# One batch of six token tiles for GT's last blocks, in a kernel that mixes linear attention with a gated linear unit

## The chip, the cores and the metric

The kernel runs on one core of one Trainium2 chip. The metric is the device time of one launch in microseconds (us), smaller is better. The engines are called PE (TensorE), ACT (ScalarE), DVE (VectorE), POOL (GpSimd) and SP (SyncE, which here only starts transfers). SP and POOL each start the transfers of one queue.

## The reference, cut to what matters

The input x has 2048 tokens of 640 values. One branch is linear attention with 32 heads of 20 values, the other a gated linear unit with an inner width of 1536; a gate per token mixes the two.

```python
phi = lambda t: where(t > 0, t + 1, exp(t)) + 1e-6
kv  = einsum("bhsd,bhse->bhde", phi(k), v)
z   = einsum("bhsd->bhd", phi(k))
num = einsum("bhqd,bhde->bhqe", phi(q), kv)
den = einsum("bhqd,bhd->bhq", phi(q), z) + 1e-6
a   = (num / den) @ wo
b   = (sigmoid(x @ w_gate) * (x @ w_up)) @ w_down
g   = sigmoid(sum(x * gate_w))
return g * a + (1 - g) * b
```

All of it is in 32 bit.

## The kernel before, in words

**Arithmetic.** Each operand of a product is split into a high and a low part (names in h and l: xth and xtl, woh and wol). `mm3` makes a product from three matmuls, at lines L407, L408 and L409 of the profile: high by high, low by high, high by low. ACT writes the high part (L420) and DVE subtracts to get the low part (L424). The large products use seven forms, sums of blocks of the operands, in place of eight block products; such sums of weights are made on DVE (the wst, qraw rows), split, and stored to DRAM by POOL (wq, wf, wd) for later use.

**k and GT.** v is never formed. Phase 1 goes through four chunks c = 0 to 3 of two blocks of 256 tokens. For each block PE makes k, ACT and DVE apply phi (tiles kr and kb, tag "kr", five buffers), and the split gives token tiles tok (`token_tile`, L492), which hold x and phi(k), high and low, for 128 tokens. POOL adds phi(k) to zacc by an accumulating transfer. `GTBatch` (L1013) adds x^T phi(k) over its token tiles, in seven units u, each in its own PSUM bank (five of 512 columns, one of 384 and one of 256), and `out` adds the bank to gt in SBUF on DVE. `batches` gives each chunk the blocks whose tiles are batched, and block 7 has a batch of its own, glast. `gt_turn` and `gt_back` then turn the columns of gt that stand past the 512th, through DRAM.

**From GT to m.** For six groups of heads hg, `kv_part` makes kv = Wv^T GT in ten matmul records (L1619; wv_sb, three buffers, loaded by `load_mv`), and DVE keeps the blocks of its heads (kvt, kvh, kvl). `wo_split` makes woh and wol from wo_sb (two buffers, `load_mo`), and asks for the load of hg+2. `m_part` multiplies kv by Wo and copies the bank to ms, with ACT, or for hg 4 with DVE (L866). These parts are spread over the slots of `q_phase(1, ...)`, which computes phi(q) for half of the columns (units ch, cc, dd with weights ws, wu, wg), by the list `extra`.

**The order.** The class `Order` (L31) plans the program at build time: pieces of ACT and DVE work wait in lists (the "qw" items among them, which sum and split the weights of the q and down products), and `fill`, `need` and `run` put them between PE's units. The order that results is fixed on each engine. An engine waits for the semaphores of its next instruction and holds back all that stands behind it, and so does SP with its loads. `queue_s` (L1320) splits the weights ws; behind the second half of each split `order.then(load_w)` places the next load of a wst tile, which has two buffers.

**Queues and PSUM.** PSUM has tiles by tag: ch, cc, dd, rot. A tile can only be written anew when its reader (ACT or DVE) is done.

Of the kernel before, what the change touches and what calls it, by code (L numbers as in the profile page):

```python
# [7 lines left out]
F32 = mybir.dt.float32  # L8
F32R = mybir.dt.float32r
# [5 lines left out]
P = 128  # L15
# [359 lines left out]
def gated_mix_kernel(ctx: ExitStack, tc: tile.TileContext, xt, xn, wk, wv, wo, wst_q, wst_f, out_t):  # L375
# [115 lines left out]

    def token_tile(dt=F32R):  # L492

        early = len(tok_n) % 6 < 4
        tok_n.append(0)
        return p1.tile([P, 4, D], dt, name="tok", tag="toka" if early else "tokb", bufs=4 if early else 2)

    p1.tile([P, HW], F32, name="first", tag="ta", bufs=2)
    warm = nc.const_aps.tensor(1.0, (P, 512), mybir.dt.bfloat16)
# [180 lines left out]
    chunks[0].b12 = (b12h, b12l)  # L680
    xt_dram = dram.tile([P, 4, 2, 2, CW], F32, name="xt_dram")
    p1.tile([P, 48], F32, name="shift")
    st = [token_tile(F32).rearrange("p a b -> p (a b)") for _ in range(2)]
    wk_st = [st[k // 3][:, k % 3 * 2 * HW:(k % 3 + 1) * 2 * HW] for k in range(KC)]
    k3h, k3l = (p1.tile([P, 2, HW], F32R, name=n, tag="kr", bufs=5) for n in ("k3h", "k3l"))
    p1.tile([P, 472], F32, name="space")

    nc.scalar.dma_start(wk_st[0][:, :HW], wk[:P, :HW])
    for k in range(KC):
# [434 lines left out]
        g.part(u, 0, 2, "rot" if u % 2 else "dd")  # L1124
        order.fill()
    order.slack(False)
    batches = {1: [1, 2], 2: [3, 4], 3: [5, 6]}

    for c in range(1, 4):
        ck = chunks[c]  # L1130
        if c == 1:
            queue_qw(2)
        a, b = KBlock(2 * c), KBlock(2 * c + 1)
        for n in range(1, 6):
            order.need((ck, n))
            if c == 1 and n >= 3:
                order.need(("ks", (1, 0, 2)[n - 3]))
            getattr(a, f"s{n}")()
            getattr(b, f"s{n}")()
            for _ in range(({1: 1, 2: 1, 3: 1, 5: 1}, {3: 2, 4: 2, 5: 2})[c - 2].get(n, 0) if c > 1 else 0):  # L1140
                order.run("qw")
        order.need((ck, 6))
        if c == 1:
            order.need(("ks", 5))
        if c == 2:
            chunks[c + 1].load()
        elif c == 3:
            nx = [Chunk(1, i, None, i * CW, xst_v, (b12h, b12l)) for i in range(2)]
            nx[0].load()
        if c == 1:  # L1150
            order.need(("xn", 1))
        queue_xn(2 * c)
        a.s6()
        a.s7()
        a.sum_b()
        a.phi_a()
        b.s6()
        a.phi_b()
        order.need(("pk", 2 * c - 1))
        k_split(tok(2 * c, 0))  # L1160
        b.s7()
        b.sum_b()
        k_split(tok(2 * c, 1))
        if c == 3:
            order.need("qw")
            qs_cm.__exit__(None, None, None)
            pa_cm.__exit__(None, None, None)
            px_cm = tc.tile_pool(name="px", bufs=1, side="right", reuse_waits="tile")
            px = px_cm.__enter__()
            xf = XForms(px, TG)  # L1170
            pg_cm = tc.tile_pool(name="pg", bufs=1, side="right", reuse_waits="tile")
            pg = pg_cm.__enter__()
            pz_cm = tc.tile_pool(name="pz", bufs=1, side="right", reuse_waits="tile")
            pz = pz_cm.__enter__()
            z = pz.tile([P, 8, CW], F32, name="xz", tag="ws")
            z0 = m1_tile("ma", "xm")[:, :2 * CW].rearrange("p (k c) -> p k c", c=CW)
            nx[1].x = (Rows((0, 2, z0), (2, KC, z[:, 0:3])), z[:, 3:8])
            nx[1].load(((0, 0, 2), (0, 2, KC), (1, 0, KC)))
            W, WT = {}, {}

            def wg_tile():
                return pg.tile([P, 2, D], F32R, name="wg", tag="wg", bufs=2)

            def put(n, i, t):
                WT[n, i] = t
                W[n, i] = [t[:, c] for c in range(2)]

            def store_w(n, i):

                key = n[::2] + (i,)  # L1190
                w_dram[key] = dram.tile(list(WT[n, i].shape), F32, name="w%s%d%d" % key)
                gp.dma_start(w_dram[key], f32(WT[n, i]))

            def wg_split(n, src):
                put(n, 0, wg_tile())
                split(*W[n, 0], src)
                if n[0] == "f" or n[2] == 0:
                    order.then(lambda: store_w(n, 0))
            nx[0].f = nx[1].f = xf
            put(("q", 1, 2), 0, wg_tile())  # L1200
            sp.dma_start(f32(WT[("q", 1, 2), 0]), w_dram["q", 2, 0])
        g = GTBatch(c, batches[c])
        if c > 1:
            order.need(("xn", 2 * c))
        if c == 1:
            chunks[1].store_t(1, 0)
        elif c < 3:
            chunks[c + 1].queue()
        else:
            queue_xn(7)  # L1210
        first = 4 if c == 1 else 3
        for u in range(first):
            g.part(u, 0, 2, ("rot", "dd", "ch", "cc")[u])
            if c == 1 and u == 0:
                order.need(("xn", 2))
                chunks[1].store_t(2, 3)
                chunks[2].queue()
            if u == (c == 1):
                b.phi_a()
            if u == 1 + (c == 1):  # L1220
                b.phi_b()
                order.ahead(5)
        queue_split(2 * c + 1)
        if c < 3:
            queue_xn(2 * c + 1)
        else:
            w_stage = m1_tile("ma", "w0")
            sp.dma_start(w_stage, wst_q[:, KC - 1])
            queue_forms(nx)
        for u in range(NU):  # L1230
            g.part(u, 2 if u in g.ps else 0, len(g.tiles), ("rot", "dd", "ch", "cc", "dd", "rot", "rot")[u])
            order.fill()
            if u in (2, 3, 4, 6):
                order.run("qw")
            if c == 2 and u == NU - 1:
                queue_ls()
    order.need(("xn", 7))
    glast = GTBatch(4, [7])
    tags = ["ch", "dd", "dd", "cc", "cc", "rot", "ch"]

    for u in (KC, KC + 1, 0):
        glast.part(u, 0, 2, tags[u])
    order.add(0, v_cost(D), gt_turn, "turned", first=True)
    for u in range(1, KC):
        glast.part(u, 0, 2, tags[u], out=False)
        order.fill()
        if u == 1:
            wg_split(("q", 1, KC - 1), w_stage)
        elif u == 3:
            glast.out(1)  # L1250
    p1_tail = [lambda u=u: glast.out(u) for u in range(2, KC)] + [lambda: order.need("turned")]
    p1_cm.__exit__(None, None, None)

    pw_cm = tc.tile_pool(name="pw", bufs=1, side="right", reuse_waits="tile")
# [291 lines left out]
            for g in gs2:  # L1546
                order.add(0, v_cost(TG), lambda g=g, u=u: one(g, u), "den", lambda g=g, u=u: order.when(st[g, u]) + 1.5, chain=True)

    sp.t = max(sp.t, z_started[-1][0])
    load_w()  # L1550
    mp_cm = tc.tile_pool(name="mp", bufs=1, reuse_waits="tile")
    mp = mp_cm.__enter__()
# [6 lines left out]
    def load_mv(hg):  # L1559
        if hg < NHG:  # L1560
            c0, w = hg_slice(hg)
            v = mp.tile([P, KC, bdn], F32, name="wv_sb", tag="wv_sb", bufs=3)
            sp.dma_start(v[:, :, :w], wv.rearrange("(k p) c -> p k c", p=P)[:, :, c0:c0 + w])
            MV[hg] = v

    def load_mo(hg):
        if hg < NHG:
# [46 lines left out]
    def kv_part(hg, tag="ch"):  # L1614
        c0, w = hg_slice(hg)
        v = MV[hg]
        ps = ps_tile(tag)
        for m in range(KC):
            nc.tensor.matmul(ps[:w, :w], v[:, m, :w], gt[:, m, c0:c0 + w], start=(m == 0), stop=(m == KC - 1))  # L1619
        order.on_pe(10, 2 * bdn)  # L1620
        kvt = mp.tile([bdn, bdn], F32, name="kvt", tag="kvt", bufs=2)
        vec2(kvt[:w, :w], ps[:w, :w], bd.rearrange("p b c -> p (b c)")[:w, :w], OP.mult, "p")
        kvh = mp.tile([bdn, bdn], F32R, name="kvh", tag="kvh", bufs=3)
        kvl = mp.tile([bdn, bdn], F32R, name="kvl", tag="kvl", bufs=3)
        vec_copy(kvh[:w, :w], kvt[:w, :w])
        vec2(kvl[:w, :w], kvt[:w, :w], f32(kvh[:w, :w]), OP.subtract)
        KV[hg] = (kvh, kvl)
        load_mv(hg + 3)
# [15 lines left out]
        queue_wo(hg + 2)  # L1644

    load_mv(0)
    sp.t = max(sp.t, order.pe + P_LAG)
    load_mv(1)
    load_mv(2)
    load_mo(0)  # L1650
    load_form(("q", 1, 2), 2)
    load_mo(1)
    load_form(("q", 1, 2), 1)

    down_pool, down_cms = [], []
# [823 lines left out]
    extra[13].append(lambda: order.need(("wg", ("f", 1, 0)), False))  # L2479
    extra[13].append(lambda: order.need(("w", ("f", 1, 0), 0), False))  # L2480
    extra[14].append(lambda: order.need(("w", ("f", 1, 0), 1), False))
    for hg, (j, t) in enumerate(((1, "rot"), (1, "rot"), (3, "cc"), (6, "rot"), (9, "rot"), (10, "rot"))):
        extra[j].append(lambda hg=hg, t=t: kv_part(hg, t))
    extra[8].append(gt_back)
    extra[12].append(z_perm)
    extra[15] += [z_sum, m_close]
    q = q_phase(1, lambda k: [(b12h[:, k], b12l[:, k])], extra)
# [524 lines left out]
def _layout(inputs):  # L3012
# [8 lines left out]
    wk = wqkv[:, D:2 * D]  # L3021
    wk = np.concatenate([wk[:, :HALF], gw, gw, wk[:, HALF:], gw, gw], axis=1)

    def cols(w):
        return np.ascontiguousarray(w).reshape(KC, P, FC, P).transpose(2, 1, 0, 3).reshape(FC, P, D)

    wst_f = np.stack([cols(inputs["B_w_gate"]), cols(inputs["B_w_up"]),
                      np.ascontiguousarray(inputs["B_w_down"]).reshape(FC, P, D)], axis=2)
    arrays = {
        "xt": xt, "xn": x, "wk": wk, "wv": wqkv[:, 2 * D:],  # L3030
        "wo": np.ascontiguousarray(inputs["A_wo"]), "wst_q": wst_q, "wst_f": wst_f,
    }
    return {k: np.ascontiguousarray(v) for k, v in arrays.items()}
# [15 lines left out]
```

## Time and profile before

| | us |
|---|---|
| median of 3 runs | 727.34 |
| lowest and highest run | 726.14, 727.4 |
| the profiled execution | 729.87 |
| span of its trace (first to last instruction) | 728.0 |
| PE busy | 719.7 |
| DVE busy | 587.0 |
| ACT busy | 370.5 |
| POOL busy | 116.4 |

The profiled execution is one execution of its own, slower than the three timed runs. In the rows of the timeline stand the start from the span's beginning in us, the duration, the engine, the line and operation, the tiles out<-in, the shape, the count, and in brackets the idle time before the instruction and what ended it. In the rows of waits stand the waiting engine and tile, the releaser, and then the total us, the number of times and the longest. In the rows of windows stand the stretch, its length, then for each engine the busy time with a count, PEclk (the granted TensorE clock, 1.00 is full speed), the share of the DMA engines, and GB/s. Names are as the program has them, with buffer numbers left out.

### The profile page before, as it was taken

The numbers are of one execution on the slowest core, as the hardware profiler recorded it, in microseconds if no ns is written. First come the engines' busy times: TensorE is split into PE (matmuls) and PEld (weight loads), VectorE is DVE, ScalarE is ACT, GpSimd is POOL, SyncE is SP. The second block draws the span as 40 slices with busy tenths as digits, with TensorE's granted clock in tenths as the row PEclk, the third lists the DMA queues.
The fourth block names the chain that finished last, engine by engine and source line by source line (L and its number), as shares of the span: only waits on it lengthen the run. The fifth ranks groups of instructions, "written<-read, shape, count | busy, mean of one in ns | idle before, by whom it ended". The sixth has DMA issues, their size and how long they took to land.

```text
span 728.0 us, 9897 instructions
## 1 busy us (share of the span) xinstructions
PE 719.7 (99%) x3395; PEld 607.4 (83%) x3395; DVE 587.0 (81%) x1016; ACT 370.5 (51%) x685; POOL 116.4 (16%) x189
## 2 busy tenths in 40 slices
PE   9999999998999999999999999999999999999998
PEld 8999998887888888888888888888888888888886
DVE  6898887986678889898989977347696968799895
ACT  5784749166556763635354754355423241444451
POOL 0211012222320221311211134001010101002300
PEclk9999999999999999999999999999999999999999
DMA  7677679798867866767677979968989895959957
GB/s 250 166 207 202 178 183 295 196 294 277 295 225 274 317 229 241 259 222 274 265 295 283 297 270 345 413 245 280 346 267 308 258 392 178 408 215 337 220 104 236
DMA packets 81960, 191.93 MB, mean 264 GB/s; under 512 B 12234, under 2 KB 40346, under 8 KB 78198
## 3 DMA queue, kind: packets, MB, share of 16 engines
q1 hardware_dynamic: 60726, 117.72, 49.6%
q0 software_dynamic: 20896, 73.36, 30.2%
q8 instruction: 26, 0.43, 0.2%
q14 instruction: 24, 0.20, 0.1%
q10 hardware_dynamic: 288, 0.23, 0.1%
HBM read 113.46 MB, written 75.52 MB: 260 GB/s over the span
## 4 chain that ended last, share of the span: by engine, by line
PE 90%; DVE 4%; issue 2%; DMA 2%; POOL 1%; ACT 0%; SPq 0%; DVEq 0%; POOLq 0%; ACTq 0%
PE ch L407 10%; PE ch L409 10%; PE ch L408 10%; PE cc L407 8%; PE cc L408 8%; PE cc L409 8%; PE dd L407 6%; PE dd L408 6%; PE dd L409 6%; PE rot L407 5%; PE rot L409 5%; PE rot L408 5%; DMA qraw<-wst_f 1%; DVE xtl L424 1%; DVE gt L424 1%
## 5 line engine op out<-in xcount | busy, mean ns | idle before, releaser
L420 ACT ACTIVATE c<-ch 128x512 f32<-128x512 f32 x54 | 32.2, 597 | 94.5 <-PE ch L409 93.7
L424 DVE TENSOR_TENSOR hf<-c,hf 128x512 fp32r<-128x512 f32 x80 | 54.4, 686 | 19.3 <-ACT hf L420 18.9
L420 ACT ACTIVATE hf<-c 128x512 fp32r<-128x512 f32 x80 | 48.9, 625 | 31.1 <-DVE c L424 31.1
L424 DVE TENSOR_TENSOR c<-cc,c 128x512 f32<-128x512 f32 x42 | 28.9, 688 | 26.9 <-PE cc L409 16.6
L407 PE MATMUL ch<-xth,ws 128*128 128x512 f32 x112 | 43.7, 390 | 0.0
L408 PE MATMUL ch<-xtl,ws 128*128 128x512 f32 x112 | 43.6, 389 | 0.0
L409 PE MATMUL ch<-xth,ws 128*128 128x512 f32 x112 | 43.6, 389 | 0.0
L424 DVE TENSOR_TENSOR c<-c,c 128x512 f32<-128x512 f32 x52 | 35.7, 687 | 3.3 <-ACT c L420 2.7
L424 DVE TENSOR_TENSOR tb<-rot,tb 128x512 f32<-128x512 f32 x56 | 36.1, 682 | 0.3 <-PE rot L409 0.3
L407 PE MATMUL dd<-xrh,wg 128*128 128x512 f32 x90 | 35.2, 391 | 0.0
L408 PE MATMUL dd<-xrl,wg 128*128 128x512 f32 x90 | 35.0, 389 | 0.0
L409 PE MATMUL dd<-xrh,wg 128*128 128x512 f32 x90 | 35.0, 389 | 0.0
L420 ACT ACTIVATE c<-dd 128x512 f32<-128x512 f32 x22 | 13.1, 596 | 41.1 <-PE dd L409 41.1
L407 PE MATMUL cc<-xbh,ws 128*128 128x512 f32 x84 | 33.0, 393 | 0.0
L408 PE MATMUL cc<-xbl,ws 128*128 128x512 f32 x84 | 32.8, 390 | 0.0
L409 PE MATMUL cc<-xbh,ws 128*128 128x512 f32 x84 | 32.7, 389 | 0.0
L424 DVE TENSOR_TENSOR tb<-dd,tb 128x512 f32<-128x512 f32 x36 | 24.7, 686 | 9.3 <-PE dd L409 9.3
L420 ACT ACTIVATE dd<-ch 128x512 f32<-128x512 f32 x22 | 12.8, 582 | 35.9 <-PE ch L409 35.9
L424 DVE TENSOR_TENSOR tb<-cc,tb 128x512 f32<-128x512 f32 x36 | 24.5, 685 | 1.9 <-PE cc L409 1.9
L424 DVE TENSOR_TENSOR wst<-wst 128x256 f32<-128x256 f32 (+1 forms) x65 | 24.6, 396 | 1.4
L409 PEld LDWEIGHTS ch<-xth,ws 128*128 128x128 f32 x112 | 21.0, 188 | 4.7 <-DVE ws L424 0.3
L408 PEld LDWEIGHTS ch<-xtl,ws 128*128 128x128 f32 x112 | 21.0, 188 | 4.3
(690 smaller groups left out, 2332.7 us busy)
## 6 DMA issues: line engine op xcount, KB each, us to landing
wf<-ws POOLq DMA_DIRECT2D x12, 1152.0 KB, 7.4
ws<-wf SPq DMA_DIRECT2D x11, 1152.0 KB, 8.5
wst<-wst_f SPq DMA_DIRECT2D x12, 640.0 KB, 5.0
wf<-wg POOLq DMA_DIRECT2D x12, 640.0 KB, 6.6
wd<-wd POOLq DMA_DIRECT2D x12, 640.0 KB, 7.7
wg<-wf SPq DMA_DIRECT2D x12, 640.0 KB, 6.8
wf<-wd SPq DMA_DIRECT2D x10, 640.0 KB, 11.1
xnst<-xn SPq DMA_DIRECT2D x16, 320.0 KB, 4.2
```

Source lines behind the costliest of these rows:

```text
L407: nc.tensor.matmul(out, l_hi, r_hi, start=first, stop=False, skip_group_check=True)
L408: nc.tensor.matmul(out, l_hi, r_lo, start=False, stop=False, skip_group_check=True)
L409: nc.tensor.matmul(out, l_lo, r_hi, start=False, stop=last, skip_group_check=True)
L420: nc.scalar.activation(out, src, fn, **kw)
L424: nc.vector.tensor_tensor(out, a, b, op=op)
```

## The change

The two last batches of GT, one of four token tiles (blocks 5 and 6) and one of two (block 7), are one batch of six, whose seven units stay in seven PSUM banks: first the first two tiles for all units, then the second two, then the last two. So that memory serves, the token tiles are split into three tags, and the results of k (tag "kr") lie between them; what reuses this memory later (mp: woh, wol, kvt, kvh, kvl) lies where kr lay. Wv is laid out on the host by groups of heads, so that a load of wv_sb reads one run per partition. The loads of wo for hg 0 and 1 stand ahead of those of ws and wu, with other times for the planner (sp.t). Two of the "qw" items of chunk 3 come after phi of block a. The kv_part of hg 4 and 5 and gt_back have earlier slots.

```diff
-        early = len(tok_n) % 6 < 4
+        tag, n = (("toka", 1), *[("tokb", 3)] * 3, *[("tokc", 2)] * 2)[len(tok_n) % 6]
         tok_n.append(0)
-        return p1.tile([P, 4, D], dt, name="tok", tag="toka" if early else "tokb", bufs=4 if early else 2)
+        return p1.tile([P, 4, D], dt, name="tok", tag=tag, bufs=n)
...
-    batches = {1: [1, 2], 2: [3, 4], 3: [5, 6]}
+    batches = {1: [1, 2], 2: [3, 4], 3: [5, 6, 7]}
...
-            for _ in range(({1: 1, 2: 1, 3: 1, 5: 1}, {3: 2, 4: 2, 5: 2})[c - 2].get(n, 0) if c > 1 else 0):
+            for _ in range(({1: 1, 2: 1, 3: 1, 5: 1}, {5: 2})[c - 2].get(n, 0) if c > 1 else 0):
                 order.run("qw")
...
         a.phi_a()
+        if c == 3:
+            order.run("qw")
+            order.run("qw")
...
+        if c == 3:
+            for u in range(first, NU):
+                g.part(u, 0, 2, ("cc", "dd", "rot", "cc")[u - first])
+                order.fill()
+            freed = [order.pe + P_LAG]
         for u in range(NU):
-            g.part(u, 2 if u in g.ps else 0, len(g.tiles), ("rot", "dd", "ch", "cc", "dd", "rot", "rot")[u])
+            g.part(u, 2 if u in g.ps else 0, 4, ("rot", "dd", "ch", "cc", "dd", "rot", "rot")[u])
...
-    glast = GTBatch(4, [7])
-    tags = ["ch", "dd", "dd", "cc", "cc", "rot", "ch"]
-
-    for u in (KC, KC + 1, 0):
-        glast.part(u, 0, 2, tags[u])
+    freed.append(order.pe + P_LAG)
+    order.need(("pk", 7))
+
+    for u in (KC, KC + 1, 1):
+        g.part(u, 4, 6)
     order.add(0, v_cost(D), gt_turn, "turned", first=True)
-    for u in range(1, KC):
-        glast.part(u, 0, 2, tags[u], out=False)
+    for u in (0, 4, 2, 3):
+        g.part(u, 4, 6, out=False)
...
-    p1_tail = [lambda u=u: glast.out(u) for u in range(2, KC)] + [lambda: order.need("turned")]
+    p1_tail = [lambda u=u: g.out(u) for u in (4, 2, 3)] + [lambda: order.need("turned")]
...
-            sp.dma_start(v[:, :, :w], wv.rearrange("(k p) c -> p k c", p=P)[:, :, c0:c0 + w])
+            sp.dma_start(v, wv[:, KC * c0:KC * (c0 + w)])
...
     load_mv(0)
-    sp.t = max(sp.t, order.pe + P_LAG)
     load_mv(1)
     load_mv(2)
     load_mo(0)
+    load_mo(1)
+    sp.t = max(sp.t, freed[1])
     load_form(("q", 1, 2), 2)
-    load_mo(1)
     load_form(("q", 1, 2), 1)
...
-    for hg, (j, t) in enumerate(((1, "rot"), (1, "rot"), (3, "cc"), (6, "rot"), (9, "rot"), (10, "rot"))):
+    for hg, (j, t) in enumerate(((1, "rot"), (1, "rot"), (3, "cc"), (6, "rot"), (6, "rot"), (8, "rot"))):
         extra[j].append(lambda hg=hg, t=t: kv_part(hg, t))
-    extra[8].append(gt_back)
+    extra[5].append(gt_back)
```

The order moves at three places of which the prediction speaks. The first is ACT in chunk 3: kb is a result of k of block b, ch its PSUM bank, qp a form of the weights, tok a token tile. Before:

```order
L420 ACTIVATE kb<-ch_1160 128x322
L420 ACTIVATE kb<-ch_1163 128x322
L420 ACTIVATE qp<-qraw 128x256 x2
L420 ACTIVATE kb<-ch_1160 128x322
L420 ACTIVATE kb<-ch_1163 128x322
L420 ACTIVATE qp<-qraw 128x256 x2
L420 ACTIVATE tok<-xnst 128x640 x2
```

and now:

```order
L420 ACTIVATE kb<-ch_1161 128x322
L420 ACTIVATE kb<-ch_1164 128x322
L420 ACTIVATE kb<-ch_1161 128x322
L420 ACTIVATE kb<-ch_1164 128x322
L420 ACTIVATE tok<-xnst 128x640 x2
L420 ACTIVATE ke<-ta 128x320
```

The four qp forms have gone from among the copies of kb; they stand behind phi of block a.

The second is the SP queue from the loads of Wv and Wo to the first weights of the gated linear unit (wst<-wst_f). Before:

```order
L364 DMA wo_sb<-wo 100x640 x2
L364 DMA wv_sb<-wv 128x5x100
L364 DMA wst<-wst_f 128x1280
L364 DMA wo_sb<-wo 100x640 x2
L364 DMA wst<-wst_f 128x1280 x2
```

and now:

```order
L364 DMA wo_sb<-wo 100x640
L364 DMA wv_sb<-wv 128x500
L364 DMA wo_sb<-wo 100x640
L364 DMA wst<-wst_f 128x1280
L364 DMA wo_sb<-wo 100x640
L364 DMA wst<-wst_f 128x1280 x2
```

The first wst<-wst_f stood behind the loads of wo for hg 2 and 3 alone; it now stands behind that for hg 4 too, which takes the buffer of hg 2.

The third is ACT in the stage that makes m, where ms is the copy of a bank of m, c and qe copies of banks of q, and wg, ws splits of weights. Before:

```order
L420 ACTIVATE woh<-wo_sb 100x640 x2
L420 ACTIVATE c_1881<-ch_1629 128x512
L420 ACTIVATE ms<-dd_1891 100x320
L420 ACTIVATE ms<-dd_1896 100x320
L420 ACTIVATE gt<-back 128x4x5x32
L420 ACTIVATE qe<-c_1881 128x512
L420 ACTIVATE c_1881<-c_1881 128x512
L420 ACTIVATE qe<-ch_1629 128x512
L420 ACTIVATE qr<-ch_1629 128x512
L420 ACTIVATE woh<-wo_sb 100x640
L420 ACTIVATE wg<-wst 128x640
```

and now:

```order
L420 ACTIVATE woh<-wo_sb 100x640
L420 ACTIVATE ws<-wst 128x512
L420 ACTIVATE woh<-wo_sb 100x640
L420 ACTIVATE wg<-wst 128x640
L420 ACTIVATE c_1883<-ch_1616 128x512
L420 ACTIVATE ms<-dd_1896 100x320
```

The split wg<-wst stood behind the copy c<-ch of this bank, and now stands ahead of it; one of the ws splits has come down between the two woh.

More of the change, by code (lines that the diff above doesn't have):

```diff
@@ L682, in gated_mix_kernel @@
     p1.tile([P, 48], F32, name="shift")
-    st = [token_tile(F32).rearrange("p a b -> p (a b)") for _ in range(2)]
+    st = [token_tile(F32).rearrange("p a b -> p (a b)")]
+    k3h, k3l = (p1.tile([P, 2, HW], F32R, name=n, tag="kr", bufs=5) for n in ("k3h", "k3l"))
+    p1.tile([P, 88], F32, name="space")
+    st.append(token_tile(F32).rearrange("p a b -> p (a b)"))
     wk_st = [st[k // 3][:, k % 3 * 2 * HW:(k % 3 + 1) * 2 * HW] for k in range(KC)]
-    k3h, k3l = (p1.tile([P, 2, HW], F32R, name=n, tag="kr", bufs=5) for n in ("k3h", "k3l"))
-    p1.tile([P, 472], F32, name="space")
+    p1.tile([P, 384], F32, name="space2")
     nc.scalar.dma_start(wk_st[0][:, :HW], wk[:P, :HW])
@@ L1237, in gated_mix_kernel @@
     order.need(("xn", 7))
-    glast = GTBatch(4, [7])
-    tags = ["ch", "dd", "dd", "cc", "cc", "rot", "ch"]
-    for u in (KC, KC + 1, 0):
-        glast.part(u, 0, 2, tags[u])
+    freed.append(order.pe + P_LAG)
+    order.need(("pk", 7))
+    for u in (KC, KC + 1, 1):
+        g.part(u, 4, 6)
     order.add(0, v_cost(D), gt_turn, "turned", first=True)
-    for u in range(1, KC):
-        glast.part(u, 0, 2, tags[u], out=False)
+    for u in (0, 4, 2, 3):
+        g.part(u, 4, 6, out=False)
         order.fill()
-        if u == 1:
+        if u == 0:
             wg_split(("q", 1, KC - 1), w_stage)
-        elif u == 3:
-            glast.out(1)
-    p1_tail = [lambda u=u: glast.out(u) for u in range(2, KC)] + [lambda: order.need("turned")]
+        elif u == 2:
+            g.out(0)
+    p1_tail = [lambda u=u: g.out(u) for u in (4, 2, 3)] + [lambda: order.need("turned")]
     p1_cm.__exit__(None, None, None)
@@ L1547, in queue_dens @@
                 order.add(0, v_cost(TG), lambda g=g, u=u: one(g, u), "den", lambda g=g, u=u: order.when(st[g, u]) + 1.5, chain=True)
-    sp.t = max(sp.t, z_started[-1][0])
+    sp.t = max(sp.t, freed[0])
     load_w()
@@ L1561, in load_mv @@
             c0, w = hg_slice(hg)
-            v = mp.tile([P, KC, bdn], F32, name="wv_sb", tag="wv_sb", bufs=3)
-            sp.dma_start(v[:, :, :w], wv.rearrange("(k p) c -> p k c", p=P)[:, :, c0:c0 + w])
-            MV[hg] = v
+            v = mp.tile([P, KC * bdn], F32, name="wv_sb", tag="wv_sb", bufs=3)[:, :KC * w]
+            sp.dma_start(v, wv[:, KC * c0:KC * (c0 + w)])
+            MV[hg] = v.rearrange("p (k c) -> p k c", c=w)
     def load_mo(hg):
@@ L1618, in kv_part @@
         for m in range(KC):
-            nc.tensor.matmul(ps[:w, :w], v[:, m, :w], gt[:, m, c0:c0 + w], start=(m == 0), stop=(m == KC - 1))
+            nc.tensor.matmul(ps[:w, :w], v[:, m], gt[:, m, c0:c0 + w], start=(m == 0), stop=(m == KC - 1))
         order.on_pe(10, 2 * bdn)
@@ L3022, in _layout @@
     wk = np.concatenate([wk[:, :HALF], gw, gw, wk[:, HALF:], gw, gw], axis=1)
+    wv = wqkv[:, 2 * D:].reshape(KC, P, D).transpose(1, 0, 2)
+    wv = np.concatenate([wv[:, :, a * DH:b * DH].reshape(P, -1) for a, b in zip(HG, HG[1:])], axis=1)
     def cols(w):
@@ L3029, in _layout @@
     arrays = {
-        "xt": xt, "xn": x, "wk": wk, "wv": wqkv[:, 2 * D:],
+        "xt": xt, "xn": x, "wk": wk, "wv": wv,
         "wo": np.ascontiguousarray(inputs["A_wo"]), "wst_q": wst_q, "wst_f": wst_f,
```

## The prediction

> **What bounds the kernel now.** I read the shares of the engines and the chain that ended last first, to see which engine sets the end, and then the waits of that engine.
>
> ```profile
> span 728.0 us, 9897 instructions
> PE 719.7 (99%) x3395; PEld 607.4 (83%) x3395; DVE 587.0 (81%) x1016; ACT 370.5 (51%) x685; POOL 116.4 (16%) x189
> PE 90%; DVE 4%; issue 2%; DMA 2%; POOL 1%; ACT 0%; SPq 0%; DVEq 0%; POOLq 0%; ACTq 0%
> ```
>
> TensorE (PE) is busy for 99% of the span, and 90% of the chain is its own. The change leaves its 3321 ordered rows and their shapes alone, so it can gain only where PE stands still. The waits of PE, with what ended them, are few:
>
> ```profile
> PE dd L407 <- DVE ms L866: 2.3, 1, 2.3
> PE ch L407 <- ACT kb L420: 0.9, 1, 0.9
> PE dd L407 <- DVE c L424: 0.9, 1, 0.9
> ```
>
> The timeline of PE places them. In each pair below the second row carries its idle time and releaser in brackets; from the first row's start a matmul at full clock takes 0.15 us (320 columns) or 0.23 us (512 columns), as the steps from row to row beside them show.
>
> ```profile
> 108.61 0.31 PE L408 MATMUL ch<-ksl,xth 128*128 128x322 f32 x1
> 108.75 0.31 PE L409 MATMUL ch<-ksh,xtl 128*128 128x322 f32 x1
> 109.96 0.42 PE L407 MATMUL ch<-k2h,xth 128*128 128x322 f32 x1 [0.90 <-ACT kb L420]
> 160.37 0.31 PE L409 MATMUL dd<-woh,kvl 120*120 120x320 f32 x1
> 161.54 0.41 PE L407 MATMUL dd<-woh,kvh 120*120 120x320 f32 x1 [0.87 <-DVE c L424]
> 162.07 1.04 PE L1619 MATMUL rot<-gt,wv_sb 128*100 128x100 f32 x10
> 162.90 0.48 PE L407 MATMUL cc<-xth,ws 128*128 128x512 f32 x1
> 167.28 0.47 PE L407 MATMUL ch<-xth,wu 128*128 128x512 f32 x1
> 179.45 0.39 PE L408 MATMUL ch<-xtl,ws 128*128 128x512 f32 x1
> 179.68 0.40 PE L409 MATMUL ch<-xth,ws 128*128 128x512 f32 x1
> 182.33 0.39 PE L407 MATMUL dd<-woh,kvh 100*100 100x320 f32 x1 [2.25 <-DVE ms L866]
> ```
>
> The windows around the third stall show the granted clock (PEclk):
>
> ```profile
> 179.70:182.30 2.60, 0.38 (x2) 0.00 (x0) 2.53 (x8) 1.74 (x3) 0.13 (x1) 1.00 0.62 201
> 183.80:187.10 3.30, 3.30 (x10) 2.56 (x8) 2.14 (x4) 1.22 (x3) 1.55 (x3) 0.50 0.73 208
> ```
>
> After that stall PE runs 3.30 us at a clock of 0.50, so half of it, about 1.6 us, is lost a second time.
>
> **What the change takes away.** Start to start, less one matmul: 109.96-108.75-0.15 = 1.06 us; 161.54-160.37-0.15 = 1.02 us; 182.33-179.68-0.23 = 2.42 us. The first matmul after each stands 0.1 longer. With the slow clock: 1.16+1.12+2.5+1.6 = 6.4 us.
>
> The first stall goes because ScalarE's copies kb<-ch stood behind two qp forms, which waited for sums of qraw, and these for a load:
>
> ```profile
> 107.43 1.80 DVE L424 TENSOR_TENSOR qraw<-qraw 128x256 f32<-128x256 f32 x4 [2.31 <-DMA qraw<-wst_f]
> 108.86 0.72 ACT L420 ACTIVATE qp<-qraw 128x256 fp32r<-128x256 f32 x2 [3.77 <-DVE qraw L424]
> 160.06 0.82 DVE L424 TENSOR_TENSOR ws<-wst,ws 128x640 fp32r<-128x640 f32 x1 [0.81 <-ACT ws L420]
> 160.80 0.68 DVE L424 TENSOR_TENSOR c<-dd,c 128x512 f32<-128x512 f32 x1
> ```
>
> In the new order the four kb copies come first and the qp forms after phi of chunk 3. The second stall (VectorE's c<-dd, 160.80, stood behind a ws split that waited for ScalarE) goes because VectorE now has the sum ahead of both ws splits. The third was VectorE's ms copies, which began at 181.79 for banks that PE had filled before the row of 179.45; they were last in a queue of VectorE that had waited on ScalarE's woh, and this on a late wo_sb load:
>
> ```profile
> 173.06 0.74 ACT L420 ACTIVATE woh<-wo_sb 100x640 fp32r<-100x640 f32 x1 [2.34 <-DMA wo_sb<-wo]
> 181.79 0.88 DVE L866 COPY ms<-dd 100x320 f32<-100x320 f32 x2
> ```
>
> From the first wg row on VectorE now has 18 instructions up to these copies, some 9.2 us (four of 640 columns at 0.75 from start to start, as 160.06 to 160.80 shows, five of 512 at 0.6, 3.2 for the small ones and the five sums of wst), and PE 10.97 us (182.33-167.28-2.42, less the two kv_parts of 0.83 us that now lie before it), so even with both starting late together PE finds the bank free. I count all three as gone.
>
> **What costs nothing.** Merging the batches removes seven VectorE additions to gt, five of 512 columns at 0.68 and two smaller, some 4 us in all:
>
> ```profile
> 140.72 0.68 DVE L424 TENSOR_TENSOR gt<-dd,gt 128x512 f32<-128x512 f32 x1
> 144.56 0.68 PE L1619 MATMUL rot<-gt,wv_sb 128*120 128x120 f32 x5
> ```
>
> PE had no wait there, so none of it is on the path. What hides the reordered work is PE's own queue: the first kv_part, at 144.56 in the trace and 143.4 with the first stall gone, needs gt whole. The xz loads that feed VectorE just ahead are issued later, since POOL's accumulations of z now stand ahead of stores that these loads wait for. I put VectorE's end of gt at 141 to 142.5, which leaves 1 to 2 us; without that cover it would cost up to 2 us. The six loads of Wv in longer runs (wv_sb) and the earlier wo loads save time only on queues that PE doesn't wait for; no wait of PE above names them, and I take zero.
>
> **What it adds: a wait on ScalarE.** On the SP queue the first GLU load wst<-wst_f now stands behind the wo_sb load of group 4. That load needs the buffer of group 2, so it waits until VectorE has made wol of group 2; before, wst was issued at 157.56, ahead of it. And on ScalarE the split wg<-wst now stands ahead of the copy c<-ch, which empties the bank that PE's next unit (ch<-xth,wu) fills. The rows of before:
>
> ```profile
> 157.56 0.61 SPq L364 DMA_DIRECT2D wst<-wst_f  x1
> 165.02 1.75 SPq L364 DMA_DIRECT2D wo_sb<-wo  x2
> 166.82 18.90 SPq L364 DMA_DIRECT2D wst<-wst_f  x2
> 159.28 1.26 ACT L420 ACTIVATE ws<-wst 128x640 fp32r<-128x640 f32 x2 [1.29 <-DVE xtl L424]
> 163.40 1.36 ACT L420 ACTIVATE woh<-wo_sb 100x640 fp32r<-100x640 f32 x2
> 164.17 0.83 DVE L424 TENSOR_TENSOR wol<-wo_sb,woh 100x640 fp32r<-100x640 f32 x1 [0.58 <-ACT woh L420]
> 166.61 0.60 ACT L420 ACTIVATE c<-ch 128x512 f32<-128x512 f32 x1 [1.85 <-PE ch L409]
> 173.70 0.72 ACT L420 ACTIVATE wg<-wst 128x640 fp32r<-128x640 f32 x1
> ```
>
> Issue. ScalarE's first woh of 100 rows came 4.1 us after ws. In the new order one ws split (0.6) leaves that stretch, one gt<-back copy (0.7) enters it, and VectorE's release comes about 0.4 earlier: woh near 162.8. VectorE's wol is ready 0.77+0.83 = 1.6 later, near 164.4 (with the ws split gone before it); SP then issues wo_sb and, some 0.4 later (an issue of wst is itself 0.61 long), wst: 164.8.
>
> Landing. These are three loads of a wst tile, each by its own view (issue to landing), the median of the kernel, and a store of POOL:
>
> ```profile
> DMA to landing us min/median/max: 5.7/5.7/5.7
> DMA to landing us min/median/max: 9.8/9.8/9.8
> DMA to landing us min/median/max: 4.1/4.1/4.1
> wst<-wst_f SPq DMA_DIRECT2D x12, 640.0 KB, 5.0
> 162.38 0.56 POOL L364 DMA_DIRECT2D wq<-ws  x1 [0.34 <-DVE ws L424]
> ```
>
> The first is the load of 157.56, the second that of 166.82, which shared the engines with POOL's stores from 162.38 on, the third the last one before them, issued at 132.77. In the new order this store comes near 165.7, just behind the wst load. I take 5.7, from the same place and with a store behind it; the bounds are 4.1 and 9.8.
>
> Price. ScalarE takes 0.72 and 0.60 for wg and c, so PE resumes 1.32 after the landing. PE wants that unit at 167.28, less the two earlier stalls (2.28), plus the two kv_parts moved ahead of it (2 x 0.83, from 162.07 to 162.90): 166.65. The stall is 164.8 + 5.7 + 1.3 - 166.65 = 5.2 us, between 3.6 and 9.3. It is longer than the 2.42 us behind which the clock fell to 0.50, so I add such a dip again: 1.6, between none and one twice as long.
>
> [...]
>
> **Sum.** -6.4 + 5.2 + 1.6 = +0.4 us on a profiled execution of 729.87 us, whose span is 728.0; the median of the runs is 727.34, 2.5 below the profiled time, and I carry the difference over: 727.34 + 0.4 = 727.7.
>
> **The rivals.** Differences under 0.2% (1.45 us) count as no change.
>
> *A. The load comes in time.* If the buffer is free sooner than my walk has it, or the landing is as short as 4.1 with no dip, the gain shows. For it speaks that the sums on VectorE are fewer by 4 us, and that each step of my walk is a hand estimate; against it, that SP's position behind wo_sb is fixed, that PE would need the landing at 166.65-1.32 = 165.3, and that no load lands 0.5 us after issue. Without any stall: 727.34-6.4 = 720.9; with 3.6 and no dip: 724.5. Landing at 5.0 without a dip gives 4.5-6.4 = -1.9, 725.4.
>
> *B. The load is starved (slower).* The wst load shares the DMA engines with POOL's 1152 KB store wq<-ws, as the load of 166.82 did, and takes 9.8: stall 9.3, and 9.3+1.6-6.4 = +4.5, 731.8. It decides from a landing of 6.8 on (6.8-0.5+1.6-6.4 = +1.5). For it speaks the store at about the same time; against it, that wst goes about 0.9 us ahead of it, where the 9.8 load went 4.4 behind.
>
> [...]
>
> *C. Late data for gt.* xz comes so late that the first kv_part waits 1 to 2 us beyond its cover: 0.4+1 to 0.4+2, 728.7 to 729.7, on the edge of what can be told.
>
> *D. The change doesn't do what it says.* VectorE is late all the same at the ms copies, whose slack behind the new stall is only about 1 us, and 1 to 2 us of the third stall stay: again 728.7 to 729.7.
>
> **How the numbers follow.** The forecast (landings 4.3 to 6.7 with a dip) has 0.42, A 0.27, B 0.20, C and D 0.11 together. The predicted time is the forecast's, 727.7; its own range is 726.3 to 728.7. The range of 8 in 10 must take in the nearer half of A (724.5 upwards; the tenth left out below is A without any stall) and B nearly to its end: 724.4 to 731.4. Faster has A's 0.27, the same 0.42, slower B, C and D, 0.31.
>
> **What would show it.** PE's waits lose <-ACT kb, <-DVE c and <-DVE ms; a new one, ch L407 <-ACT c or <-DMA wst, stands near 166.6, 3.6 to 9.3 us long, with ScalarE's wg<-wst waiting for DMA wst just ahead and a clock of 0.50 behind it. SP issues wst near 164.8. If wst is issued before 161, or ScalarE's wg split waits less than 1 us, the forecast is wrong and A holds; if the rot<-gt,wv_sb row waits for VectorE's gt, it is C.

## The result, and the profile after

| | before | changed |
|---|---|---|
| median of 4 runs each, us | 727.09 | 731.74 |
| lowest and highest, us | 726.14, 727.4 | 731.48, 732.55 |
| ratio | | 1.0068, 95% interval 1.0051 to 1.0085 |
| profiled execution, us | 729.87 | 731.82 |
| its span, us | 728.0 | 730.1 |

The changed kernel is 0.7% slower: 4.65 us between the medians, though only 2.1 between the two spans. One later execution, of the layout of Wv alone, took 1701.59 us at full clock for a reason that nothing here shows, and its ratio leaves it out. The page of the changed kernel:

```profile
span 730.1 us, 9886 instructions
...
PE 719.4 (99%) x3395; PEld 607.4 (83%) x3395; DVE 583.3 (80%) x1009; ACT 371.0 (51%) x685; POOL 117.1 (16%) x189
```

VectorE does 3.7 us less (587.0 before, the additions of the batch that is gone) and the end does not come sooner. PE's waits:

```profile
PE ch L407 <- ACT c L420: 6.1, 1, 6.1
...
PE dd L407 <- DVE c L424: 0.3, 1, 0.3
```

The waits for ScalarE's kb and VectorE's ms are gone, that for c is 0.3 in place of 0.9, and one wait of 6.1 us has come. The timelines of SP, ScalarE and PE around it, and the view of the wst load:

```profile
164.08 0.30 SPq L364 DMA_DIRECT2D wo_sb<-wo  x1
164.44 0.33 SPq L364 DMA_DIRECT2D wst<-wst_f  x1
```

The view of the wst load (issue to landing):

```profile
DMA to landing us min/median/max: 7.2/7.2/7.2
```

ScalarE's timeline:

```profile
163.56 0.74 ACT L420 ACTIVATE woh<-wo_sb 100x640 fp32r<-100x640 f32 x1
171.68 0.74 ACT L420 ACTIVATE wg<-wst 128x640 fp32r<-128x640 f32 x1 [7.37 <-DMA wst<-wst_f]
172.32 0.58 ACT L420 ACTIVATE c<-ch 128x512 f32<-128x512 f32 x1
```

PE's timeline:

```profile
165.79 1.04 PE L1629 MATMUL rot<-gt,wv_sb 128*100 128x100 f32 x10
172.95 0.79 PE L407 MATMUL ch<-xth,wu 128*128 128x512 f32 x1 [6.11 <-ACT c L420]
173.54 0.63 PE L408 MATMUL ch<-xtl,wu 128*128 128x512 f32 x1
```

SP, which waited 9.2 us for VectorE's wol, issues the wo_sb load at 164.08, wst behind it at 164.44, and wst lands 7.2 later. ScalarE waits 7.37 us with the split of wg at its head; the copy c<-ch stands behind it, and PE's next unit behind that. The last kv_part takes 0.83, so PE wanted the unit at 166.62: it stood still for 172.95-166.62 = 6.33 us. Then the clock is low, as the windows show (the columns as before, PEclk third from the end):

```profile
166.80:171.40 4.60, 0.04 (x1) 0.00 (x0) 0.00 (x0) 0.00 (x0) 0.00 (x0) 1.00 1.02 382
171.50:178.20 6.70, 5.25 (x12) 4.13 (x13) 4.15 (x8) 4.77 (x10) 1.64 (x3) 0.50 0.63 203
178.30:181.00 2.70, 2.70 (x16) 2.32 (x15) 1.85 (x3) 1.11 (x3) 0.54 (x1) 1.00 0.95 361
```

From 171.5 to 178.2 PE has half its clock. The 12 matmuls from 172.95 to 178.2 take 5.25 us in place of 12 x 0.23 = 2.76: 2.5 us lost. Stall and slow clock are 8.8 us in this execution.

### The profile page after: what moved, and what is told of

It is laid out like the page before. It is cut to its first block, busy times and chain, and to the rows that moved or that the text cites. A ratio compares the mean times of both kernels' runs of the same rounds, so it can differ in the third digit from the quotient of the medians.

```text
span 730.1 us, 9886 instructions
## 1 busy us (share of the span) xinstructions
PE 719.4 (99%) x3395; PEld 607.4 (83%) x3395; DVE 583.3 (80%) x1009; ACT 371.0 (51%) x685; POOL 117.1 (16%) x189
## 4 chain that ended last, share of the span: by engine, by line
PE 93%; DMA 3%; DVE 2%; ACT 1%; SPq 0%; issue 0%; ACTq 0%; DVEq 0%
PE ch L407 11%; PE ch L408 11%; PE ch L409 11%; PE cc L407 9%; PE cc L408 9%; PE cc L409 9%; PE dd L407 6%; PE dd L408 6%; PE dd L409 6%; PE rot L407 5%; PE rot L409 5%; PE rot L408 5%; DMA ws<-wq 1%; DMA wst<-wst_f 1%; PE dd L2787 1%; DVE xtl L424 1%
## 5 line engine op out<-in xcount | busy, mean ns | idle before, releaser
L407 PE MATMUL ch<-xth,wu 128*128 128x512 f32 x56 | 22.5, 402 | 6.1 <-ACT c L420 6.1
```

Of the source, the lines that this page charges most:

```text
L407: nc.tensor.matmul(out, l_hi, r_hi, start=first, stop=False, skip_group_check=True)
```

## The experiments

All ratios are to the kernel before, timed beside it on the same chip.

**Was the first profile of before typical?** It took 2.5 us more than the median. The kernel before, unchanged, was profiled again.

> The kernel before, once more, for a second profile of it. The first profiled execution took 729.87 us, 2.5 above the median. Theory: those 2.5 us are the third stall (2.42 us at dd<-woh,kvh behind DVE ms) and the slow clock behind it (1.6 us), which ordinary executions have only in part; so this execution takes about 727, and the wait of PE for DVE ms is under 1.5 us or has no stretch at 0.50 behind it. Rival: the third stall is in every execution (2.3 to 2.5 us, with the slow clock), and the difference lies elsewhere or is that of one execution.

It took 726.62 us, with a span of 724.9. PE's waits:

```profile
PE dd L407 <- DVE ms L866: 1.9, 1, 1.9
PE dd L407 <- DVE c L424: 0.9, 1, 0.9
...
PE cc L407 <- DVE c L424: 0.5, 1, 0.5
```

Neither theory had it whole. The first stall, which I had counted at 1.16 us, is not there. The timelines of VectorE and ScalarE say why, and the windows show the third stall:

```profile
104.57 1.80 DVE L424 TENSOR_TENSOR qraw<-qraw 128x256 f32<-128x256 f32 x4 [0.15 <-DMA qraw<-wst_f]
```

ScalarE's timeline:

```profile
107.50 0.44 ACT L420 ACTIVATE kb<-ch 128x322 f32<-128x322 f32 x1 [0.78 <-PE ch L409]
```

The windows:

```profile
178.00:180.10 2.10, 0.19 (x2) 0.02 (x1) 2.03 (x7) 1.35 (x3) 0.18 (x1) 1.00 0.49 151
180.10:190.00 9.90, 9.40 (x42) 7.58 (x43) 8.15 (x13) 5.70 (x10) 4.40 (x9) 1.00 0.80 288
```

The same program, but VectorE waited 0.15 us for the load of qraw, not 2.31, and ScalarE's kb waited for PE, not PE for it. The third stall is there (1.91 us of wait), but nothing behind it runs at 0.50: 9.40 of 9.90 us busy at full clock, the rest being a wait of 0.5 that the first profile does not have. So the theory was right on the slow clock and wrong on the stall's size; of the 6.4 us that I counted as removable, 1.16 + 1.6 are not in this execution.

For the slow clock the timed runs say how often it comes. Each lists the mean granted clock of its span: 0.998 in the first profile of before, which has one stretch at 0.50, and 1.000 in the second, which has none. Of the 72 runs of the kernel before that were timed beside the experiments, 25 have 0.998 or less, with a median of 728.3 us; the other 47 have 726.85. So a clock as low as with that stretch comes in about a third of the executions, which are about 1.5 us longer; over all of them that is about 0.5 us, not 1.6. Where in the span the clock was low, these runs don't list.

**The load in its old place.** In the changed kernel the wst load alone moves ahead of the wo_sb load of group 4.

```diff
     def wo_split(hg):
...
+        if hg == 2:
+            order.then(load_w)
         order.then(lambda: load_mo(hg + 2))
...
                 order.then(lambda: store_w(n, 2))
-                order.then(load_w)
+                if n != ("q", 1, 0):
+                    order.then(load_w)
```

> The changed kernel with one load moved: wst<-wst_f stands ahead of the wo_sb load of group 4 on the SP queue, so it waits for no wol. Theory (the new stall is this load's place in the queue): wst is issued near 153, right behind wv_sb at 152.74, lands by 160, ScalarE's wg split waits for nothing, the stall of 6.3 us at ch<-xth,wu and the slow clock behind it (2.4 us) are gone: 731.7-8.7 = 723.0; if woh of group 4 then waits for its own load, up to 2.7 more, 725.7. Rival (the stall is ScalarE's or VectorE's own order, or the slow clock has another cause): it stays within 1 us of 731.7.

Median 727.19 of 11 runs, ratio 1.0000 (0.9986 to 1.0014). SP issued wst at 153.76; ScalarE's wg split waited for nothing. PE's waits, and two rows of ScalarE's timeline:

```profile
PE ch L407 <- ACT c L420: 2.3, 2, 1.8
...
PE dd L407 <- DVE ms L868: 0.7, 1, 0.7
...
```

ScalarE's timeline:

```profile
169.35 0.74 ACT L420 ACTIVATE woh<-wo_sb 100x640 fp32r<-100x640 f32 x1 [2.23 <-DMA wo_sb<-wo]
...
177.31 0.74 ACT L420 ACTIVATE woh<-wo_sb 100x640 fp32r<-100x640 f32 x1 [4.00 <-DMA wo_sb<-wo]
```

The 6.1 us are gone, though wg's split still stands ahead of the copy c<-ch, so the load's place made the stall. No slow clock follows in this execution (mean granted clock 1.000); 3 of the 11 runs have 0.995 to 0.997. What the theory held open came, larger: the two next wo_sb loads are late, and the copies of c behind woh of group 5 make PE wait 1.8 us. The time is that of the kernel before, not 723.

**Does POOL's store starve the load?** In the changed kernel the 1152 KB store wq<-ws goes behind the store of wg, which needs the wst load.

```diff
-                order.then(lambda: store_w(n, 2))
+                if n != ("q", 1, 0):
+                    order.then(lambda: store_w(n, 2))
...
                     order.then(lambda: store_w(n, 0))
+                if n == ("f", 1, 0):
+                    order.then(lambda: store_w(("q", 1, 0), 2))
```

> The changed kernel with one store moved: POOL's 1152 KB store wq<-ws stands behind the store wf<-wg, which needs the wst load, so it no longer runs beside that load. Theory (starved by the store): the wst load lands in 4.1 to 5.0 us in place of 7.2, the stall falls from 6.3 to 3.2 to 4.2 us, and the time to 728 to 729. Rival (the load takes 7 us there by itself): landing 7.0 to 7.4 and 731.7 again.

Median 730.95 of 5 runs, ratio 1.0050 (1.0037 to 1.0063). The wait of PE and the landing of wst:

```profile
PE ch L407 <- ACT c L420: 5.1, 2, 4.6
```

The view of the wst load (issue to landing):

```profile
DMA to landing us min/median/max: 5.7/5.7/5.7
```

The store costs the load 1.5 us (7.2 to 5.7), and the stall falls by as much (6.1 to 4.6). That is part of it, not most: without the store the load still takes 5.7, more than the 4.1 to 5.0 expected, and the stall stays. In the time the gain can't be told: 1.0050 against 1.0068 and 1.0059 of the changed kernel, by intervals that overlap.

**Two qw items of chunk 3 alone**, in the kernel before.

```diff
-            ... {3: 2, 4: 2, 5: 2})[c - 2]
+            ... {5: 2})[c - 2]
...
         a.phi_a()
+        if c == 3:
+            order.run("qw")
+            order.run("qw")
```

> The kernel before with one part of the change: two qw items of chunk 3 come after phi of block a. Theory: the first stall (PE ch<-k2h behind ACT kb, 1.16 us) is gone and nothing behind it gives the time back: 727.1-1.2 = 725.9. Rival: the later stalls are set by loads, which don't come earlier, and take the 1.2 us back: 727.1.

Median 726.36 of 11 runs, ratio 0.9983 (0.9974 to 0.9993), as the theory had it. But its profile has other stalls than the first two profiles of before:

```profile
PE dd L407 <- DVE c L424: 1.4, 1, 1.4
...
PE rot L407 <- DVE gt L424: 0.5, 1, 0.5
...
```

No wait for ScalarE's kb, but none for VectorE's ms either, which this edit doesn't name, and a new one for gt. The edit does not stand alone: the planner moved later work with it, among it a split of ws (behind two ms copies now) and that of wg (ahead of a woh now) on ScalarE. Since the first stall was not in the second profile of before, I don't put the 0.17% down to it. Part of it may be the slow clock: none of the 11 runs has a granted clock of 0.998 or less, against 8 of the 21 of before on that chip.

**A third buffer for wo_sb** in the changed kernel. The planner then also puts the split of wg eight rows later on ScalarE.

```diff
-            o = mp.tile([bdn, D], F32, name="wo_sb", tag="wo_sb", bufs=2)
+            o = mp.tile([bdn, D], F32, name="wo_sb", tag="wo_sb", bufs=3)
...
-        order.then(lambda: load_mo(hg + 2))
+        order.then(lambda: load_mo(hg + 3))
...
     load_mo(1)
+    load_mo(2)
```

> The changed kernel with a third buffer for wo_sb, so that the load of group 4 no longer waits for wol of group 2 (all else that moves follows from the planner: wg's split stands eight rows later on ScalarE, behind the copies of q). Theory (the new stall is the wst load's place behind a load that waits for VectorE): wst is issued near 160 to 164, ScalarE's wg split holds nothing that PE needs, no wait of PE for ACT c at ch<-xth,wu, no slow clock: 6.3+2.6 us less than the changed kernel, 723 to 724; in ratio to the kernel before 0.994 to 0.996. Rival (the load is late whatever stands ahead of it, since POOL's stores take the engines): a stall of 1 to 3 us stays behind ScalarE, ratio 0.998 to 1.002, as with the load moved alone (1.0000).

Median 724.81 of 12 runs, ratio 0.9970 (0.9958 to 0.9981), a little less than expected. The only wait of PE that its list shows (at the program's start), and the timelines of SP and ScalarE:

```profile
PE rot L502 <- PEq L3054: 0.8, 1, 0.8
```

SP's timeline:

```profile
164.27 0.30 SPq L364 DMA_DIRECT2D wo_sb<-wo  x1
164.63 15.88 SPq L364 DMA_DIRECT2D wst<-wst_f  x3
```

ScalarE's timeline:

```profile
171.25 0.74 ACT L420 ACTIVATE wg<-wst 128x640 fp32r<-128x640 f32 x1 [1.02 <-DMA wst<-wst_f]
```

The buffer did not bring the load forward: wst goes at 164.63, behind the wo_sb load of group 5 now. It lands only 0.4 us earlier than in the changed kernel (the split starts at 171.25, not 171.68), and ScalarE waits for it 1.02 us, with nothing behind it that PE needs. So a load that late costs nothing in itself; it costs by what stands behind its split.

**The buffer and the load**: the same, with wst placed ahead of the wo_sb loads of groups 3 to 5 (one more `load_w()` behind the loads of ws and wu, and none behind the split of ws).

> The same, and the wst load placed ahead of the wo_sb loads of groups 3 to 5. Theory: wst is issued before 146 and landed before 155, neither it nor a wo_sb load is waited for; no wait of PE over 1 us between 100 and 190; ratio to the kernel before 0.992 to 0.995. Rival (POOL's stores wf<-wg and wq<-ws, now earlier, starve the loads that come next): a wait of 1 to 2 us stays near 178 to 183, ratio 0.997 to 1.000.

Median 724.8 of 7 runs, ratio 0.9964 (0.9949 to 0.9979). wst was issued at 139.61. PE's waits:

```profile
PE ch L407 <- ACT c L420: 0.6, 1, 0.6
PE dd L407 <- DVE c L424: 0.6, 1, 0.6
PE dd L408 <- DVE wol L424: 0.5, 1, 0.5
```

The waits are as the theory had them, all under 1 us, and the ratio between the two forecasts, no different from that of the buffer alone.

**The copy first.** In the changed kernel the split of wg is held back by one place, so that c<-ch (and VectorE's sum of c) goes ahead of it; the load stays.

```diff
-            lambda: order.when(W_AT[n]) if n in W_AT else 1e9,
+            lambda: order.when(W_AT[n]) + (13.0 if n == ("f", 1, 0) else 0.0) if n in W_AT else 1e9,
```

> The changed kernel with ScalarE's copy c<-ch (and VectorE's sum of c) ahead of the split of wg; the load as it was. Theory (a late load holds whatever stands behind its split): PE's wait at ch<-xth,wu goes, and one of about 4 us comes at dd<-woh,kvh some 4 us later, since ScalarE's ms copies and woh, and VectorE's wol, stand behind the split; 2 to 3 us less than the changed kernel, ratio to before 1.002 to 1.004. Rival (the order of the two on ScalarE is the cause, the load is not late for anything else): no stall over 1 us there, ratio 0.994 to 0.997.

Median 728.52 of 10 runs, ratio 1.0021 (1.0012 to 1.0031), as the theory had it. PE's waits and ScalarE's split:

```profile
PE dd L407 <- DVE ms L868: 1.7, 1, 1.7
PE dd L407 <- ACT ms L420: 1.7, 1, 1.7
...
```

ScalarE's timeline:

```profile
171.26 0.74 ACT L420 ACTIVATE wg<-wst 128x640 fp32r<-128x640 f32 x1 [5.83 <-DMA wst<-wst_f]
```

ScalarE still waits 5.83 us. The stall at ch<-xth,wu has gone to dd<-woh,kvh, some 6 us later, where PE waits 1.7 us for the ms copies behind the split (I had 4), and 1.7 more for VectorE's ms. There is no slow clock in this execution, the fastest of the ten; 7 of the ten have a mean granted clock of 0.997 or 0.998.

**The layout of Wv alone**, in the kernel before.

```diff
-            v = mp.tile([P, KC, bdn], F32, name="wv_sb", tag="wv_sb", bufs=3)
-            sp.dma_start(v[:, :, :w], wv.rearrange("(k p) c -> p k c", p=P)[:, :, c0:c0 + w])
+            v = mp.tile([P, KC * bdn], F32, name="wv_sb", tag="wv_sb", bufs=3)[:, :KC * w]
+            sp.dma_start(v, wv[:, KC * c0:KC * (c0 + w)])
```

> The kernel before with Wv laid out by groups of heads and nothing else by hand; the planner then has VectorE's sum of c ahead of the ws splits, and the wst load behind the wo_sb loads of groups 4 and 5, with ScalarE's wg split late. Theory (that load's place costs only where its split stands ahead of a copy that PE waits for): no new stall, the second stall (1.1 us) gone, ratio 0.998 to 0.999. Rival (the place in the queue is enough): a stall of 3 to 6 us, ratio 1.004 to 1.008.

Median 724.5 of 9 runs, ratio 0.9963 (0.9949 to 0.9978): better than the theory, and as good as anything here. PE's waits and SP's rows:

```profile
PE dd L407 <- DVE ms L866: 1.0, 1, 1.0
...
PE cc L407 <- DVE c L424: 0.5, 1, 0.5
PE dd L407 <- DVE c L424: 0.3, 1, 0.3
```

SP's timeline:

```profile
162.20 3.28 SPq L364 DMA_DIRECT2D wo_sb<-wo  x2
165.53 16.95 SPq L364 DMA_DIRECT2D wst<-wst_f  x3
```

wst stands behind two wo_sb loads and goes even later than in the changed kernel, and no stall of its own comes of it. The second stall falls from 0.9 to 0.3 and the third from 1.9 to 1.0.

**The changed kernel again**, for a second profile, and **the changed kernel with the old layout of Wv** (the diff above, reversed; apart from these loads every engine has the same order).

> The changed kernel once more, beside the next three on one chip, for a second profile. Theory: the stall at ch<-xth,wu is in every execution (5.5 to 6.5 us), with at least one stretch of 3.4 us at a clock of 0.50 behind it; ratio to before 1.005 to 1.008. Rival: it depends on the execution; a profile without it, and runs that spread by 5 us.

> The changed kernel with the old layout of Wv; the rest of the change as it is, and wst and wg's split at the same places. Theory (the layout of Wv acts through the order that the planner makes, not through the transfers): stall and time as in the changed kernel, ratio to before 1.004 to 1.008, not over 0.2% from it. Rival (the longer runs free the DMA engines): 0.3% slower than the changed kernel, 1.009 to 1.011.

The changed kernel had a median of 731.54 us in 6 runs, ratio 1.0059 (1.0046 to 1.0072); with the old layout 732.25 in 5, 1.0066 (1.0054 to 1.0078). For the changed kernel, the wait, then the unit behind the stall and the windows around it:

```profile
PE ch L407 <- ACT c L420: 6.1, 1, 6.1
```

PE's timeline:

```profile
173.21 0.80 PE L407 MATMUL ch<-xth,wu 128*128 128x512 f32 x1 [6.07 <-ACT c L420]
```

The windows:

```profile
166.00:172.50 6.50, 1.14 (x12) 0.97 (x10) 0.00 (x0) 0.56 (x1) 0.52 (x1) 0.78 0.93 320
172.50:176.00 3.50, 2.79 (x7) 2.22 (x8) 3.26 (x6) 3.01 (x7) 1.09 (x2) 0.50 0.44 150
176.00:180.00 4.00, 4.00 (x20) 3.42 (x19) 2.45 (x6) 2.12 (x5) 1.09 (x2) 0.94 0.99 318
```

The view of the wst load (issue to landing):

```profile
DMA to landing us min/median/max: 7.2/7.2/7.2
```

The wait with the old layout:

```profile
PE ch L407 <- ACT c L420: 5.7, 1, 5.7
```

The stall is there in both profiles of the changed kernel, with the same landing. The slow clock is as long as in the first, but it lies earlier. An estimate, with the clock at 1.00 or at 0.50 as in the windows of the first: a mean of 0.78 over 6.50 us means 0.50 for 2.9 of them, so it begins near 169.6; a mean of 0.94 over 4.00 us means 0.5 at 0.50, so it ends near 176.5. That is some 6.9 us, of which 3.6 lie in the stall, and PE loses half of the 3.3 behind it: 1.6 us, not 2.5. With the old layout the load lands after 6.8, and the times differ by less than their intervals: the layout changes nothing that can be told as long as the order is kept. This speaks for its having acted, in the run before, through the order that the planner makes with it; no run has the kernel before with that order and the old layout.

**Wv and the qw items**, in the kernel before, without and with a third buffer for wo_sb (the diffs above, together).

> The kernel before with the new layout of Wv and the two qw items behind phi of block a. Theory (the two parts remove different stalls): the sum of both, 0.9963 - 0.0017 = 0.9946, 0.993 to 0.996. Rival (the first stall is in a part of the executions only, and the two share the rest): as the layout alone, 0.996 to 0.998.

> The same with a third buffer for wo_sb (and with it the wo loads earlier). Theory (the third stall is the late wo_sb loads): no wait for DVE ms over 0.3 us, 0.992 to 0.995. Rival (POOL's stores make the next load late, whichever it is): no better than without the buffer, within 0.1% of it.

Medians 726.07 and 725.8 of 12 runs each, ratios 0.9978 (0.9966 to 0.9989) and 0.9980 (0.9970 to 0.9991). The gains don't add: the rivals hold in both. The waits of the second:

```profile
PE dd L407 <- DVE c L424: 1.4, 1, 1.4
...
PE rot L407 <- DVE gt L424: 0.4, 1, 0.4
```

The wait for VectorE's ms is gone, as the theory said, but not by the buffer: the first of the two has none either. The wait for c has grown from the 0.3 of Wv alone to 0.9 without the buffer and 1.4 with it.

Six versions have intervals below 1. The three best, by intervals that overlap, are the buffer (0.9970), the buffer with the load (0.9964), and the layout of Wv alone (0.9963). With the stall taken out, all that the change holds together is worth no more, as far as these intervals tell, than its smallest part. Some of these gains may be the slow clock: of the runs of the buffer (12), the buffer with the load (7) and the layout of Wv (8 that count), none has a mean granted clock of 0.998 or less, against 25 of 72 of the kernel before.

## Why the prediction was wrong

The range ended at 731.4 and the median is 731.74; the forecast was no change. The new wait was foreseen, in its place and its cause. What failed were sizes in the sum, and most of all its first term: 6.4 us taken away, where the profiles show 3.4. By its own steps:

- **The new wait: right in place and cause, too small.** wst was put at 164.8 and went at 164.44; PE was to want the unit at 166.65 and did at 166.62; 1.32 from landing to PE was 1.27 (171.68 to 172.95). The term that failed here is the landing: 5.7 taken, 7.2 measured, in two profiles. 1.5 of it is the store, by the one profile of the run that moves it. The stall is 6.33, not 5.2.
- **The slow clock: between right and too small.** 1.6 was taken from a stretch of 3.30 us at 0.50. The longer stall brings 6.7 to 6.9 us of it, partly before PE resumes: it cost 2.5 in the first profile of the changed kernel and 1.6 in the second. That the second agrees with the forecast is luck, since the stretch was twice as long as the one taken.
- **What the change takes away: the largest error.** I worked out 6.4 from one profiled execution, 2.5 us above the median, and carried the difference over unchanged. The second profile of before shows that most of the excess lay in the very stalls that I took off: the first (1.16) and the slow clock (1.6) are not in it, and the timed runs have that clock in a third of the executions. Against it the changed kernel saves the third stall (about 2.1), the wait for c behind it (about 0.7) and some 0.6 of the second: 3.4. With this, -3.4 + 6.3 + 2.5 = +5.4, against 730.1-724.9 = 5.2 between the spans. With the second profile of the changed kernel, -3.4 + 6.3 + 1.6 = +4.5, against 729.6-724.9 = 4.7. The medians are 4.65 apart.
- **The second stall** was to go whole; 0.3 us of wait stays.
- **What costs nothing: right for this kernel.** The first kv_part starts at 142.74 without a wait, and the ms copies are in time (case D did not come, nor C). That Wv's layout acts on no queue that PE waits for holds where the order is kept (1.0066 and 1.0059). What I missed is that it also moves the planner's order: alone it is worth 0.37%.
- **Rival B** named the right price, 731.8, by luck, for a reason only half right. The landing is past its deciding point of 6.8, but 7.2 and not 9.8, and by its own sum 7.2 would have given 6.7+1.6-6.4 = +1.9. The errors in the gain and in the clock made up the rest.

Not settled: why the load takes 5.7 us without that store, which part of the new order makes the gain of the layout of Wv, and how often the first stall of before is there; two profiles of it don't say.

## What to carry to other kernels

A term "what the change removes" is only as typical as the profile that it is read from: when the profiled execution is longer than the median by as much as the terms, take it again, or take the excess off the gain. The mean granted clocks of the timed runs tell, without a second profile, how often a slow clock comes (here 25 of 72). A late transfer costs by what stands behind its first reader, so look there first: with the copy c<-ch behind the split of wg, a load that landed 7.2 us after its issue cost PE 6.1; with the copy ahead of it the ratio fell from 1.0068 to 1.0021, and with nothing behind it that PE needed a wait of 1.02 us on ScalarE gave PE no wait. So put the copies that empty PSUM ahead of splits of freshly loaded weights. And an edit that only lays out a load anew can, as the two runs of the layout suggest, act through a planner's order more than through the transfer.

## What the runs showed of the hardware

Behind 2.42 us between matmuls the granted clock of the first profile of before has one stretch at 0.50, with 1.00 ahead of it and behind it:

```profile
182.40:183.70 1.30, 1.30 (x8) 1.25 (x9) 1.30 (x3) 0.65 (x2) 0.88 (x2) 1.00 0.33 126
183.90:187.10 3.20, 3.20 (x10) 2.46 (x8) 2.04 (x4) 1.12 (x3) 1.55 (x3) 0.50 0.71 199
187.30:190.00 2.70, 2.70 (x14) 2.19 (x13) 2.18 (x4) 1.01 (x3) 1.10 (x2) 1.00 1.01 369
```

It is between 3.2 and 3.6 us long (3.4 by windows of 0.1 us, from 183.8 to 187.2) and starts 1.5 us after PE resumed; the changed kernel's is between 6.7 and 6.9, about twice that, and starts 1.5 us before PE resumes in the first profile, 3.6 before in the second. From one matmul of 512 columns to the next it has 0.43 us, against 0.23 at full clock. A stall of 1.91 us in the second profile of before, and two of 1.7 in the run with the copy first, had none (the mean granted clock of both executions is 1.000). Yet 25 of 72 other executions of the one program and 7 of 10 of the other have 0.998 or less. So one and the same program lost some 1.6 us more behind the wait at dd<-woh,kvh in one execution, and nothing in another. What decides it is not shown: the timed runs list no gaps.
